# Sooner loads and one batch of logits in a convolution and mixture-of-experts kernel

## The chip, the cores and the metric

The kernel runs on one NeuronCore of a Trainium2 chip. The core has five engines with instruction streams of their own: TensorE (PE, with its weight loads shown as PEld), VectorE (DVE), ScalarE (ACT), GpSimd (POOL) and SyncE (SP, which here issues most of the loads). The metric is the device time of one launch, in microseconds (us); the figure of a kernel is the median of its runs.

## The reference

The first half is a dynamic convolution. For each of 8 x 2880 tokens with 192 channels in 8 heads, a softmax over 7 taps of `weight_gen` weights the token and its 6 predecessors:

```python
w = softmax(weight_gen)                       # (8, 2880, 8 heads, 7 taps)
x_unf = x_pad[:, idx, :].reshape(B, S, K, H, group)
out = np.einsum('bshk,bskhg->bshg', w, x_unf)
```

The second half is a mixture of 4 x 4 experts over the 23040 tokens. A softmax over 4 groups picks one group for each token, a softmax over its 4 experts picks one expert, and only that expert runs:

```python
h = np.maximum(xg[mask_e] @ w1[g, e], 0.0)    # 192 -> 1024
ye = h @ w2[g, e]                             # 1024 -> 192
out[tok_idx] = g_w * e_w * ye
```

All arrays are float32.

## The kernel before

The tokens are worked in 15 groups of 12 x 128. For a group, `load_group` loads the convolution weights (`wt`) and the inputs (`xin`); `softmax` normalises `wt`; `conv` makes the weighted sums on DVE; `route` computes the logits, picks the expert, ranks the tokens and gives each one a row in a DRAM buffer `rows`, which is sorted by expert. POOL writes the rows there by indirect DMA (`scatter_row`). After some groups `table` makes a list of blocks of one expert that are full; the ends of these rounds stand in `ROUNDS`. After the last group POOL also writes 16 blocks of padding (`rows<-pad`, line 588).

The experts run in visits, numbered from 0 in this text (the fourth is visit 3). A visit takes rows of one expert (`xb<-rows`), its first matrix (`wa`) and its second (`wc`). The first ten visits, 0 to 9, are "plain": 128 rows, float32 matmuls, and the first matrix is loaded straight into `wa`. The later ones take 256 rows and a "split" first matrix: it is loaded raw (`raw<-in_moe_w` and `raw<-w1lo`), ACT makes the high part (lines 806 and 809) and DVE the low part (line 824). For each of the three kinds of raw tile there are two, two and one buffers, so the raw tile of visit 12 is the one that visit 10 used. In the last rounds the second matrix is split as well (line 816). The last eight visits are plain again.

PE's work in a visit is `gemm1` (line 892, into `ph`), whose result ACT takes out with a relu (line 898, `hh`), and `gemm2` (line 919, into `py`), which ACT takes out (line 928) and POOL writes to `out` (line 936). Groups 0 to 4 sum the convolution in PSUM by transposing matmuls (line 319). From group 5 on DVE does the sums (lines 280 and 298), and the rows are transposed for the logits in six pairs (lines 393 and 394), each copied by ACT to a tile `xT`, of which there are two. After every second pair 8 logit matmuls follow (`logits`, line 365), with weights 32 columns wide; after the third such batch the result is copied, transposed back (line 430) and worked on by DVE.

Every engine runs its instructions in the order in which they were recorded. The code that records them is a planner: it keeps a clock for each engine (`clk`), advances it by a written cost for each step, and interleaves the visits with the steps of the convolution (`front`, `fill`, `step`) by it. Loads wait in a list `want`; `ask` puts a load there, `pump` issues those that are ready, in order, on SP. `ask_w` asks for the parts of a first matrix, `ask(n, 3)` for a second matrix, `ask(n, 0)` for the rows. `halves` (lines 623 to 636), in the early part, splits the tail rows of all first matrices through the same raw buffers and stores the low parts in DRAM.

Of the kernel before, what the change touches and what calls it, by code (L numbers as in the profile page):

```python
# [8 lines left out]
F32 = mybir.dt.float32  # L9
# [13 lines left out]
EVERY = {}  # L23
WHOLE = (99,) * 11 + (3, 0, 0)
TURNED = 10


class Slot:
# [4 lines left out]
def conv_moe_kernel(ctx: ExitStack, tc: tile.TileContext, x, wgen, w_group, w_expert, w1, w2, out):  # L33
# [5 lines left out]
    P = 128  # L39
# [163 lines left out]
    def run(eng, cost, *deps):  # L203
        clk[eng] = max([clk[eng]] + [d + HOP for d in deps]) + cost
        return clk[eng]
# [145 lines left out]
    def route(g, o):  # L351
# [26 lines left out]
        def forward():  # L378
            xTs = []
            for s2 in range(0, SG, 2):  # L380
                n, i = s2 // SC, s2 % SC // 2
                if o.chunks <= n:
                    yield Chunk(o, n + 1)
                row = xrow[n][:, s2 % SC:s2 % SC + 2, :]
                if i == 0:
                    rem = rt.tile([P, SC, HP], F32, name="rem")
                    nc.scalar.copy(out=rem, in_=xrow[n][:, :, P:D])
                    txT = run("act", 0.4, clk["dve"])
                    yield NEXT
                ttp = run("pe", 0.35, txT)  # L390
                tp = ps_t.tile([P, 3, P], F32, name="tp")
                for u in range(2):
                    nc.tensor.transpose(out=tp[:, u, :], in_=row[:, u, 0:P], identity=ident)  # L393
                nc.tensor.transpose(out=tp[:, 2, :], in_=rem[:, s2 % SC:s2 % SC + 2, :].rearrange("p s d -> p (s d)"), identity=ident)
                if len(xTs) == 2:
                    run("pe", 0.5, txT)
                    logits(s2 - 4, xTs)
                    xTs = []
                xT = rt.tile([P, 3, P], F32, name="xT", bufs=2)
                nc.scalar.copy(out=xT, in_=tp)  # L400
                txT = run("act", 0.48, ttp)
                xTs.append((xT, False))
                yield NEXT
            run("pe", 0.5, txT)
            logits(SG - 4, xTs)

        turned = 2 * g < TURNED
        if turned:
# [247 lines left out]
    def front():  # L656
# [5 lines left out]
        for g in range(ENDS[-1]):  # L662
# [2 lines left out]
            state["urgent"] = g == FIRST  # L665
            for n, c in enumerate(conv(g, o)):
                yield c
                if n in (2, 8) and 1 <= g < ENDS[-1] - 1:
                    load_group(g + 1, (n // 8,))
                if n >= (12 if state["slots"] else 4) and not o.ahead and g + 1 < ENDS[-1]:  # L670
                    o.ahead = True
                    side.append([softmax(g + 1), None])
# [288 lines left out]
    def blocks(n0, n1, paced):  # L961
        want, jobs = [], []

        def pump(upto=None):
            for a in list(want):
# [8 lines left out]
                want.remove(a)  # L974
                load(*a)

        def ask(n, part):
            if n < n1:
                want.append((n, part))

        def ask_x(n):
# [44 lines left out]
        if n0 + 2 < n1 and plain(n0 + 2):  # L1026
            ask_w(n0 + 2)
            ask(n0 + 2, 3)
        for n in range(n0, min(n0 + 3, n1)):
            ask(n, 0)  # L1030
        if n0 + 2 < n1 and not plain(n0 + 2) and (whole(n0 + 2) or whole(n0 + 1)):
# [15 lines left out]
        for i in range(len(units) + LAG):  # L1047
# [21 lines left out]
            if i < len(units):  # L1069
                n, j, u = units[i]  # L1070
                nb = blocks_of(n)
                at = j * NU + u
                end = at == nb * NU - 1
                if end and n + 3 < n1 and (plain(n + 3) or plain(n + 1)):
                    ask_w(n + 3)
                did = 0
                for job in list(jobs):
                    m, part, h = job
                    if m > n + 2 or (part == 3 and (m > n + 1 or at < LAG)):
                        continue  # L1080
                    must = end and m == n + 1
                    if not must and (did >= 1 or (m, part) in want or not ready(m)):
                        continue
                    jobs.remove(job)
                    work_split(job)
                    did += 1
                state["unit"] += 1
# [46 lines left out]
```

## Time and profile before

| | |
|---|---|
| runs | 1240.4, 1240.73 and 1241.85 us; median 1240.73 |
| profiled execution | 1243.13 us, of which 1241.5 us are the span of the trace |
| PE busy | 1190.0 us, 96% of the span |
| DVE busy | 922.6 us, 74% |
| ACT busy | 662.1 us, 53% |
| POOL busy | 428.0 us, 34% |
| DMA | 286.08 MB, 230 GB/s in the mean |

The span is read in stages. Up to about 115 us there are only convolution and routing; from there to about 239 us the plain visits run beside groups 2 to 5; from 239 to about 830 us the 256-row visits run beside the other groups; up to about 930 us the last routing follows; then come split visits alone, and plain ones at the end. Where PE is busy without a gap, PE's own instructions set the time. Where it stands, the row says in brackets for how long, and what released it. In the timeline a row is one instruction, or several equal ones that follow each other; "L892" is line 892 of the kernel before.

### The profile page before, as it was taken

To read this page: it belongs to the slowest core of one execution; us is meant where nothing else is said; L and a number is where in the kernel's file an instruction comes from. 1 tells how busy PE (TensorE), PEld (TensorE's weight loads), DVE (VectorE), ACT (ScalarE), POOL (GpSimd) and SP (SyncE) were. 2 spreads that over 40 slices of the span, in tenths; PEclk is the share of its full clock that TensorE was granted. 3 is DMA by queue.
4 is the path that set the end of the run, shared out by engine and by line. 5 is a ranking of instruction groups with operands and counts; after the bars stand their busy time and mean duration, and the time that the engine had idled before them with its cause. 6 is when DMAs were issued, how large, how long until landed. Compare 5 with 4: busy or idle time off the path is not lost.

```text
span 1241.5 us, 26600 instructions
## 1 busy us (share of the span) xinstructions
PE 1190.0 (96%) x9456; PEld 1162.9 (94%) x9456; DVE 922.6 (74%) x1582; ACT 662.1 (53%) x1242; POOL 428.0 (34%) x412
## 2 busy tenths in 40 slices
PE   5998899899999999999999999999998999999995
PEld 5887899899999999999999999999998999999995
DVE  8887678698989898898899889961255776777500
ACT  1223333455565555555656565555665777777531
POOL 3062424151626253433424342444154112211111
PEclk9999999899999999999999999999998999999998
DMA  4448988888877888797969786868569777776891
GB/s 150 137 137 245 271 289 263 251 248 268 245 259 232 274 237 265 214 295 222 282 204 301 218 279 206 238 199 259 179 188 300 226 224 232 221 224 199 233 261 43
DMA packets 181677, 286.08 MB, mean 230 GB/s; under 512 B 16084, under 2 KB 141775, under 8 KB 181280
## 3 DMA queue, kind: packets, MB, share of 16 engines
q1 hardware_dynamic: 162304, 245.09, 65.8%
q0 software_dynamic: 19232, 39.22, 9.6%
q8 instruction: 76, 1.25, 0.4%
q14 instruction: 65, 0.53, 0.1%
HBM read 240.89 MB, written 44.33 MB: 230 GB/s over the span
## 4 chain that ended last, share of the span: by engine, by line
PE 67%; issue 20%; DVE 4%; POOL 4%; DMA 3%; ACT 1%; SPq 0%; POOLq 0%; DVEq 0%; ACTq 0%
PE py L919 27%; PE ph L892 27%; POOL out L936 3%; PE pl L365 2%; PE ph L319 1%; PE py L214 1%; DVE pr L280 1%; PE py L319 1%; PE tpx L319 1%; PE tpx L868 1%; PE tpx L869 1%; PE tp L393 1%; DMA raw<-in_moe_w 1%; PE tp L374 1%; DMA wc<-in_moe_w 1%
## 5 line engine op out<-in xcount | busy, mean ns | idle before, releaser
L892 PE MATMUL ph<-xh,wa 128*128 128x256 f32 x2064 | 459.7, 299 | 0.0
L936 POOL DMA_INDIRECT out<-xb x190 | 207.2, 1090 | 657.3 <-ACT xb L928 407.5
L919 PE MATMUL py<-wc,hh 128*128 128x192 f32 x2240 | 417.7, 327 | 9.8 <-ACT xb L928 9.8
L919 PEld LDWEIGHTS py<-wc,hh 128*128 128x128 f32 x2240 | 359.9, 191 | 10.2 <-ACT xb L928 10.2
L892 PE MATMUL ph<-xlo,wa 128*128 128x256 f32 x1376 | 359.4, 283 | 0.0
L892 PEld LDWEIGHTS ph<-xh,wa 128*128 128x128 f32 x2064 | 351.0, 191 | 7.4 <-issue 5.9
L898 ACT ACTIVATE hh<-ph 128x512 f32<-128x512 f32 (+1 forms) x316 | 173.2, 548 | 317.2 <-PE ph L892 317.2
L892 PEld LDWEIGHTS ph<-xlo,wa 128*128 128x128 f32 x1376 | 262.5, 191 | 0.0
L280 DVE TENSOR_TENSOR pr<-xin,wt 128x1152 f32<-128x1152 f32 x190 | 253.6, 1351 | 6.2 <-PE tpx L319 6.1
L533 POOL DMA_INDIRECT rows<-xrow,posi x180 | 201.9, 1122 | 133.2 <-DVE posi L500 57.2
L298 DVE TENSOR_TENSOR xrow<-xrow,pr 128x1152 f32<-128x1152 f32 x120 | 162.4, 1353 | 0.6
L824 DVE TENSOR_TENSOR wa<-raw,wa 128x1024 fp32r<-128x1024 f32 x86 | 104.9, 1220 | 71.2 <-ACT wa L806 63.8
L921 PE MATMUL py<-wc,hh 128*128 128x384 f32 x400 | 122.5, 362 | 0.0
L824 DVE SCALAR_TENSOR_TENSOR hl<-ph,hh 128x512 fp32r<-128x512 f32 x100 | 69.1, 691 | 66.8 <-ACT hh L903 66.4
L922 PE MATMUL py<-wc,hl 128*128 128x192 f32 x400 | 100.8, 252 | 0.0
L806 ACT CAST wa<-raw 128x1024 fp32r<-128x1024 f32 x86 | 90.3, 1050 | 6.2 <-DMA raw<-in_moe_w 6.2
L809 ACT CAST wa<-raw 128x1024 fp32r<-128x1024 f32 x86 | 89.5, 1040 | 0.0
L928 ACT ACTIVATE xb<-py,xb 128x192 f32<-128x192 f32 x190 | 71.6, 420 | 27.3 <-PE py L919 21.5
L892 PE MATMUL ph<-xd,wa 96*128 96x128 f32 x576 | 78.8, 281 | 0.5 <-ACT xd L862 0.5
L922 PEld LDWEIGHTS py<-wc,hl 128*128 128x128 f32 x400 | 77.5, 194 | 0.0
L921 PEld LDWEIGHTS py<-wc,hh 128*128 128x128 f32 x400 | 76.2, 190 | 0.0
L892 PEld LDWEIGHTS ph<-xd,wa 96*128 96x128 f32 x576 | 75.1, 198 | 0.8 <-ACT xd L862 0.7
(165 smaller groups left out, 1291.2 us busy)
## 6 DMA issues: line engine op xcount, KB each, us to landing
wc<-in_moe_w SPq DMA_DIRECT2D x79, 768.0 KB
raw<-in_moe_w SPq DMA_DIRECT2D x86, 512.0 KB
raw<-in_moe_w SPq DMA_DIRECT2D x102, 256.0 KB
xin<-in_x SPq DMA_DIRECT2D x26, 864.0 KB
raw<-w1lo SPq DMA_DIRECT2D x86, 256.0 KB
raw<-in_moe_w SPq DMA_DIRECT2D x25, 768.0 KB
xb<-rows SPq DMA_DIRECT2D x86, 194.0 KB
wa<-in_moe_w SPq DMA_DIRECT2D x36, 384.0 KB
```

The costliest lines, as they stand in the source:

```text
L280: nc.vector.tensor_tensor(out=dst, in0=o.xin[:, c0 + k:c0 + k + SC, :].rearrange("p s (h g) -> p s h g", g=HG), in1=w4[:, c0:c0 + SC, :, k ...
L298: nc.vector.tensor_tensor(out=acc, in0=acc, in1=prs[k - 2], op=ALU.add)
L533: written_once(nc.gpsimd.indirect_dma_start(out=rows[:, :], out_offset=bass.IndirectOffsetOnAxis(ap=idx, axis=0), in_=src, in_offset=None, ...
L806: nc.scalar.copy(out=o.wa[:, 0, :], in_=o.raw[0])
L809: nc.scalar.copy(out=o.wa[:, 2, :], in_=o.raw[1])
L824: f(*a, **k)
L892: nc.tensor.matmul(ph[:, v, :], lhsT=w[:, f0:f0 + P], rhs=rhs, start=i == 0, stop=i == len(terms) - 1)
L898: nc.scalar.activation(out=hh, in_=ph, func=AF.Relu)
L919: nc.tensor.matmul(b.py[t][:, 0:D], lhsT=hh[:, v, c], rhs=wc[0][:, f, :], start=f == 0, stop=f == NFT - 1)
L921: nc.tensor.matmul(b.py[t], lhsT=hh[:, v, c], rhs=wc[f // 4][:, f % 4].rearrange("p l d -> p (l d)"), start=f == 0, stop=False)
L922: nc.tensor.matmul(b.py[t][:, 0:D], lhsT=hl[:, v, c], rhs=wc[f // 4][:, f % 4, 0, :], start=False, stop=f == NFT - 1)
L936: ins = nc.gpsimd.indirect_dma_start(out=out[:, :], out_offset=bass.IndirectOffsetOnAxis(ap=b.x.bitcast(I32)[:, t, D + 1:D + 2], axis=0), ...
```

## The change

There are four edits.

- In `front`, the weights and the first half of the inputs of the next group are asked for after the first product of a group instead of the third, for groups 2, 3 and 4. The second halves, and later groups, stay.
- In `blocks`, the second matrix of visit 3 is asked for at the start, with those of visits 0 to 2, and a set `asked` keeps it from being asked for twice.
- In `blocks`, the raw first matrices of visits 10 and 11 are asked for at the end of visits 6 and 7 instead of 7 and 8.
- In `route`, for groups 5 to 12, the first four transposed pairs go to tiles of the ring `hl` (four buffers, otherwise used early by the transposed convolution sums and late by the split visits), the last two to `xT`, and all 24 logit matmuls are issued together after the last pair.

```diff
--- before.py
+++ after.py
@@ -23,6 +23,7 @@
 EVERY = {}
 WHOLE = (99,) * 11 + (3, 0, 0)
 TURNED = 10
+BATCH = 13
 
 
 class Slot:
@@ -392,17 +393,21 @@
                 for u in range(2):
                     nc.tensor.transpose(out=tp[:, u, :], in_=row[:, u, 0:P], identity=ident)
                 nc.tensor.transpose(out=tp[:, 2, :], in_=rem[:, s2 % SC:s2 % SC + 2, :].rearrange("p s d -> p (s d)"), identity=ident)
-                if len(xTs) == 2:
+                if len(xTs) == 2 and g >= BATCH:
                     run("pe", 0.5, txT)
                     logits(s2 - 4, xTs)
                     xTs = []
-                xT = rt.tile([P, 3, P], F32, name="xT", bufs=2)
+                if g < BATCH and s2 < 8:
+                    xT = wp.tile([P, 3, P], F32, name="hl", bufs=4)
+                else:
+                    xT = rt.tile([P, 3, P], F32, name="xT", bufs=2)
                 nc.scalar.copy(out=xT, in_=tp)
                 txT = run("act", 0.48, ttp)
                 xTs.append((xT, False))
                 yield NEXT
-            run("pe", 0.5, txT)
-            logits(SG - 4, xTs)
+            run("pe", 0.25 * len(xTs), txT)
+            for q in range(len(xTs) // 2):
+                logits(SG - 2 * len(xTs) + 4 * q, xTs[2 * q:2 * q + 2])
 
         turned = 2 * g < TURNED
         if turned:
@@ -665,8 +670,9 @@
             state["urgent"] = g == FIRST
             for n, c in enumerate(conv(g, o)):
                 yield c
-                if n in (2, 8) and 1 <= g < ENDS[-1] - 1:
-                    load_group(g + 1, (n // 8,))
+                at = (0 if g < FIRST + 2 else 2, 8)
+                if n in at and 1 <= g < ENDS[-1] - 1:
+                    load_group(g + 1, (at.index(n),))
                 if n >= (12 if state["slots"] else 4) and not o.ahead and g + 1 < ENDS[-1]:
                     o.ahead = True
                     side.append([softmax(g + 1), None])
@@ -974,8 +980,11 @@
                 want.remove(a)
                 load(*a)
 
+        asked = set()
+
         def ask(n, part):
-            if n < n1:
+            if n < n1 and (n, part) not in asked:
+                asked.add((n, part))
                 want.append((n, part))
 
         def ask_x(n):
@@ -1026,6 +1035,8 @@
         if n0 + 2 < n1 and plain(n0 + 2):
             ask_w(n0 + 2)
             ask(n0 + 2, 3)
+            if n0 + 3 < n1 and plain(n0 + 3):
+                ask(n0 + 3, 3)
         for n in range(n0, min(n0 + 3, n1)):
             ask(n, 0)
         if n0 + 2 < n1 and not plain(n0 + 2) and (whole(n0 + 2) or whole(n0 + 1)):
@@ -1071,8 +1082,10 @@
                 nb = blocks_of(n)
                 at = j * NU + u
                 end = at == nb * NU - 1
-                if end and n + 3 < n1 and (plain(n + 3) or plain(n + 1)):
+                if end and n + 3 < n1 and plain(n + 3):
                     ask_w(n + 3)
+                if end and n + 4 < n1 and plain(n + 2) and not plain(n + 4):
+                    ask_w(n + 4)
                 did = 0
                 for job in list(jobs):
                     m, part, h = job
```

On SP the weights of group 4 stand as follows; `wt` and `xin` are that group's loads, `raw` and `w1lo` the loads and stores of `halves`. Before:

```order
L623 DMA raw_171<-in_moe_w 64x1024 x2
L636 DMA w1lo<-raw_170 64x1024 x2
L623 DMA raw_173<-in_moe_w 64x1024 x2
L636 DMA w1lo<-raw_172 64x1024 x2
L623 DMA raw_170<-in_moe_w 64x1024 x2
L238 DMA wt<-in_weight_gen 128x672
L248 DMA xin<-in_x 128x1728
```

Changed (the lines are those of the changed kernel, five or six higher further down):

```order
L628 DMA raw_171<-in_moe_w 64x1024 x2
L641 DMA w1lo<-raw_170 64x1024 x2
L628 DMA raw_173<-in_moe_w 64x1024 x2
L239 DMA wt<-in_weight_gen 128x672
L249 DMA xin<-in_x 128x1728
L641 DMA w1lo<-raw_172 64x1024 x2
L628 DMA raw_170<-in_moe_w 64x1024 x2
```

The two loads of group 4 have moved ahead of one store pair and one load pair. For groups 2 and 3 SP's order is the same as before.

A little later on SP come the raw first matrices of the first split visits; `raw_170` and `raw_172` are the buffers of visits 10 and 12, `raw_171` and `raw_173` those of visit 11. Before, the rows of visit 12 and then the first of visit 11:

```order
L786 ISA
L786 DMA raw_170<-in_moe_w 128x1024
L789 ISA
L789 DMA raw_172<-in_moe_w 64x1024
L789 ISA
L789 DMA raw_172<-w1lo 64x1024
L781 TENSOR_LOAD tab_1908
L781 ISA x2
L786 ISA
L786 DMA raw_171<-in_moe_w 128x1024
```

Changed, the rows of group 6's loads and of visit 11:

```order
L239 DMA wt<-in_weight_gen 128x672
L249 DMA xin<-in_x 128x1728
L787 TENSOR_LOAD tab_1908
L787 ISA x2
L792 ISA
L792 DMA raw_171<-in_moe_w 128x1024
L795 ISA
L795 DMA raw_173<-in_moe_w 64x1024
L795 ISA
L795 DMA raw_173<-w1lo 64x1024
```

Before, the load of visit 11 stands behind those of visit 12, which refill the buffers of visit 10. Changed, it stands directly behind the loads of group 6, ahead of the rows of visit 10, where the raw loads of visit 10 stood before; those have moved one visit further up.

The planner also places the last group's routing elsewhere among the visits. On POOL, the last scatters and the first block of padding; `xb` with its number is the buffer of a visit, and they go round from 158 to 165. Before:

```order
L936 DMA out<-xb_162 23040x192 x2
L533 DMA rows<-xrow,posi 188928x194 x12
L936 DMA out<-xb_163 23040x192 x2
L586 TENSOR_LOAD pfi
L586 ISA x2
L588 ISA
L588 DMA rows<-pad 128x388
```

Changed:

```order
L942 DMA out<-xb_159 23040x192 x2
L538 DMA rows<-xrow,posi 188928x194 x2
L942 DMA out<-xb_160 23040x192 x2
L538 DMA rows<-xrow,posi 188928x194 x10
L942 DMA out<-xb_161 23040x192 x2
L591 TENSOR_LOAD pfi
L591 ISA x2
L593 ISA
L593 DMA rows<-pad 128x388
```

The first padding stands behind the output of `xb_161` instead of that of `xb_163`, two visits sooner, and the output of one visit stands between the scatters.

## Rows read from the trace of the kernel before

**Rows 1.** The first part of the page (busy time, share of the span and instructions of each engine) and one line of its second part (PE's busy share in 40 equal slices of the span, in tenths).

```profile
PE 1190.0 (96%) x9456; PEld 1162.9 (94%) x9456; DVE 922.6 (74%) x1582; ACT 662.1 (53%) x1242; POOL 428.0 (34%) x412
...
PE   5998899899999999999999999999998999999995
```

**Rows 2.** Stretches of 50 us; columns: length of the stretch, then busy time and instructions of PE, PEld, DVE, ACT and POOL, the granted PE clock (1.00 is full speed), the share of time in which the DMA engines were busy, and GB/s.

```profile
100.00:150.00 50.00, 42.91 (x353) 39.75 (x351) 34.21 (x73) 15.15 (x37) 12.36 (x10) 0.93 0.86 241
...
200.00:250.00 50.00, 43.42 (x360) 41.55 (x359) 36.98 (x75) 21.15 (x45) 14.22 (x14) 0.93 0.86 259
...
300.00:350.00 50.00, 50.00 (x384) 49.16 (x386) 45.52 (x81) 29.09 (x54) 26.55 (x22) 1.00 0.82 255
...
900.00:950.00 50.00, 47.55 (x354) 46.95 (x352) 26.69 (x81) 28.11 (x50) 28.14 (x37) 0.99 0.79 247
950.00:1000.00 50.00, 49.20 (x364) 49.21 (x365) 35.41 (x51) 35.88 (x61) 10.41 (x11) 0.94 0.75 227
```

**Rows 3.** Timeline, 123 to 136 us; columns: start, length, engine (SPq is SP's DMA queue), line, operation, tiles, count, and in brackets the idle time before and what ended it.

```profile
123.22 1.25 SPq L636 DMA_DIRECT2D w1lo<-raw  x2
...
126.56 0.58 SPq L238 DMA_DIRECT2D wt<-in_weight_gen  x1
...
132.56 0.85 DVE L255 TENSOR_REDUCE m<-wt 128x96 f32<-128x672 f32 x1 [7.99 <-DMA wt<-in_weight_gen]
...
134.34 0.76 ACT L258 ACTIVATE wt<-wt 128x672 f32<-128x672 f32 x1 [5.83 <-DVE wt L257]
...
136.00 0.92 PE L919 MATMUL py<-wc,hh 128*128 128x192 f32 x4 [4.19 <-ACT xb L928]
```

**Rows 4.** The three standstills of PE and what follows each, as stretches; columns as in rows 2.

```profile
131.81:136.00 4.19, 0.00 (x2) 0.00 (x1) 3.37 (x6) 1.66 (x5) 0.00 (x0) 1.00 1.03 280
136.00:140.30 4.30, 4.30 (x22) 4.28 (x23) 4.20 (x12) 0.22 (x1) 2.66 (x2) 0.60 1.05 232
228.97:234.57 5.60, 0.01 (x2) 0.00 (x1) 1.10 (x1) 2.18 (x5) 0.00 (x0) 0.81 1.05 259
234.57:239.30 4.73, 4.73 (x18) 4.73 (x19) 4.31 (x7) 1.68 (x4) 0.97 (x1) 0.51 0.81 257
947.22:950.80 3.58, 0.33 (x2) 0.14 (x2) 1.54 (x3) 2.90 (x6) 2.55 (x3) 0.78 1.05 354
950.80:956.00 5.20, 5.20 (x22) 5.20 (x23) 2.95 (x6) 3.63 (x6) 1.26 (x2) 0.50 0.76 233
```

**Rows 5.** Timeline, 209 to 235 us, the loads of raw first matrices by SP, and the first work on visit 11's by ACT; columns as in rows 3.

```profile
209.56 1.48 SPq L786 DMA_DIRECT2D raw<-in_moe_w  x1
...
221.99 0.34 SPq L786 DMA_DIRECT2D raw<-in_moe_w  x1
...
224.84 0.35 SPq L786 DMA_DIRECT2D raw<-in_moe_w  x1
...
232.39 1.04 ACT L806 CAST wa<-raw 128x1024 fp32r<-128x1024 f32 x1 [6.17 <-DMA raw<-in_moe_w]
```

**Rows 6.** The chain of waits, early and at 285 us; columns: start, length, engine, tile, line, count. L365 are the logits; 8 matmuls are 16 instructions, 24 are 48.

```profile
110.63 1.49 PE pl L365 x48
...
284.93 0.57 PE pl L365 x16
```

**Rows 7.** Timeline of PE's weight loads: the last before and the first behind a batch of 24 logit matmuls, and the same for a batch of 8; columns as in rows 3.

```profile
211.02 1.18 PEld L214 LDWEIGHTS py<-ident 128*128 128x128 f32 x11 [0.53 <-ACT xlo L325]
...
213.82 0.31 PEld L374 LDWEIGHTS tp<-ident,hl 128*128 128x128 f32 x3 [0.20 <-issue]
...
284.55 0.14 PEld L394 LDWEIGHTS tp<-ident,rem 128*128 128x128 f32 x1
...
285.43 0.30 PEld L892 LDWEIGHTS ph<-xh,wa 128*128 128x128 f32 x2 [0.20 <-issue]
```

**Rows 8.** Timeline of POOL, ACT and PE around the padding, 928 to 951 us; columns as in rows 3.

```profile
928.87 3.27 POOL L588 DMA_DIRECT2D rows<-pad  x6
...
947.51 0.54 POOL L588 DMA_DIRECT2D rows<-pad  x1 [0.75 <-issue]
...
947.90 0.83 ACT L816 CAST wc<-raw 128x768 fp32r<-128x768 f32 x1 [6.98 <-DMA raw<-in_moe_w]
...
948.27 0.33 PE L868 MATMUL tpx<-ident,xb 128*128 128x128 f32 x1 [1.05 <-DMA xb<-rows]
950.80 0.47 PE L869 MATMUL tpx<-ident,xd 128*128 128x128 f32 x1 [2.20 <-ACT xd L852]
```

**Rows 9.** A stretch of 10 us during the padding; columns as in rows 2.

```profile
930.00:940.00 10.00, 10.00 (x80) 10.00 (x80) 7.45 (x15) 7.37 (x13) 6.28 (x11) 1.00 1.05 320
```

**Rows 10.** SP's semaphore waits at line 770, the loads of rows (count, shortest, median and longest in ns, first and last start); the first three loads of rows; the stretch from 98 to 108 us; and PE's first use of such rows.

```profile
L770 SPq EVENT_SEMAPHORE  x117: 17/28/9524, 98.3 to 1208.2; - x117
...
107.92 3.10 SPq L770 DMA_DIRECT2D xb<-rows  x3
...
98.00:108.00 10.00, 9.25 (x79) 8.54 (x80) 8.99 (x10) 3.65 (x5) 3.68 (x3) 1.00 0.88 260
...
115.36 0.43 PE L860 MATMUL tp<-ident,xb 128*96 128x128 f32 x2 [0.57 <-ACT xrow L375]
```

**Rows 11.** Waits between 240 and 900 us: who waited for whom, us in total, times, longest.

```profile
DVE wa L824 <- ACT wa L806: 51.5, 16, 10.0
```

## Prediction

> **What bounds the kernel now.** I read the page first: PE is busy 1190.0 us of a span of 1241.5, in nearly every slice 90% or more [rows 1]. So PE's own instructions set the time, and apart from start and end there is little idle time to win. The stretches of 50 us say where it is: from 300 to 350 us PE is busy without a gap, while 100 to 150, 200 to 250 and 900 to 1000 us lack 7.1, 6.6, 2.5 and 0.8 us [rows 2]. The timeline puts nearly all of the last three, and 4.2 us of the first, into three standstills, and a table of stretches gives each with what follows it: 4.19, 5.59 and 3.25 us (3.58 less the 0.33 in which PE worked) [rows 4]. Behind each one PE is busy, but at a granted clock of 0.60, 0.51 and 0.50, that is mostly or all at 1.2 instead of 2.4 GHz. At half clock the same instructions take twice as long, so these stretches hold a further loss of 4.30 x 0.40 = 1.7, 4.73 x 0.49 = 2.3 and 5.20 x 0.50 = 2.6 us.
>
> The sum below is made in the profiled execution, 1243.1 us: the span and 1.6 us around it. That is 2.4 us over the median of 1240.73; I take the 2.4 us off at the end.
>
> **The weights of group 4.** DVE waited 7.99 us for `wt`, which SP issued at 126.56 us [rows 3]. The exponential at line 258 stood next on ACT, which takes its instructions in order, so the outputs of PE behind it were not taken out, and PE stood until 136.00. In the changed order the load stands ahead of one store pair and one load pair, where SP stood at 123.22: 3.3 us sooner. The load itself has the same work queued before it, so I let all behind it come 3.3 us sooner and PE stand for about 0.9 us. Whether so short a stop still brings the slow clock, rows 3 and 4 do not tell; I take half of its 1.7 us. Term: 3.3 + 0.9 = 4.2 us. Bounds: 0, if SP reaches this place later, and 5.9, if the stop goes with its slow clock. For groups 2 and 3 the order on SP is unchanged, so the edit gives nothing there.
>
> **The second matrix of visit 3.** 768 KB more are now queued ahead of the first rows `xb`. SP's own time for it is covered: it waited up to 9.5 us, from 98.3 us on, before those rows could be issued at 107.92 [rows 10]. The transfer takes 768 KB / 260 GB/s = 3.0 us more of the DMA engines, which are 0.88 busy there. PE first uses such rows at 115.36, over 7 us behind the issue, and there it waited for ACT, not for them. I count nothing; without that cover it would be at most these 3.0 us, by pushing everything on SP back. In exchange 768 KB are gone from the stretch where `wt` was late, 1.03 to 1.05 busy [rows 4]. The Trainium skill, "DMA: Bandwidth & Descriptors", section "Queues, rings and completion order", says that each DMA engine consumes the descriptors of one issuing engine's ring in order. That rule speaks against this edit: by it the rows of visits 0 to 2 wait for the whole matrix. No row here separates the two, and by the rule the sum is the same as long as the slack at 115.36 holds.
>
> **The raw matrices of visits 10 and 11.** Before, visit 11's load stood behind that of visit 12, which had to wait until visit 10's buffers were free: SP issued these at 221.99, and visit 11's only at 224.84 [rows 5]. ACT met line 806 with nothing landed, stood 6.17 us until 232.39, and everything behind it on ACT too; PE stood 5.59 us [rows 4]. In the changed order visit 11's load stands where visit 10's stood, at 209.56, some 15 us sooner. Even a landing as slow as the 7.5 us from 224.84 to 232.39 would end at 217, long before ACT is free at 232.39 - 6.17 = 226.2. The rows and the second matrix of visit 10 stand behind one such load, as before. Those of visit 9 now stand behind visit 10's raw load, 1024 KB, at 259 GB/s [rows 2] 4.0 us of transfer; they are asked for three visits ahead, and I count nothing for them. Next in line are line 806 itself (1.04 us) and PE's own instructions. Term: 5.6 + 2.3 = 7.9 us. Bounds: 5.6, if the slow clock comes all the same, to 7.9.
>
> **Logits of groups 5 to 12.** No instruction is removed, but the 24 matmuls are in one batch. The timeline of the weight loads has both kinds: from the end of the last load before a batch of 8 (284.69) to the first behind it (285.43) 0.74 us, around a batch of 24 (212.20 to 213.82) 1.62 us [rows 7]. Three batches cost 2.22, one costs 1.62: 0.60 us a group, and 4.8 us for eight groups, since PE has no gap there [rows 2]. Bounds: 4.0 to 5.0, for the units in which the batches stand differ. The copies to `hl` and `xT` are as many as before, and the last batch waited for the last copy before, too.
>
> What a logit matmul costs inside a batch is seen in the chain: 48 instructions take 1.49 us, 31 ns each [rows 6]. The Trainium skill, "TensorE: Matmul & The Clock Gate", section "Part 3: Packing small matmuls", has matmuls in different column strips of the array run beside each other, about 4 ns apart. By that a batch of 24 would cost little more than one of 8, and a group would save 2 x 0.74 = 1.5 us instead of 0.6, eight groups 11.8. The trace shows 31 ns and not 4, so the sum goes by the row.
>
> **The padding.** This comes with the planner's new order. Before, the 16 blocks of padding were written from 928.87 to 948 us, with the DMA engines 1.05 busy [rows 8, 9]; ACT waited 6.98 us for a raw second matrix and PE 1.05 us for rows, then 2.20 for ACT. Now the first block stands two visits sooner, beside visits whose second matrices are not split and are asked for three visits ahead. It may cost nothing there: 3.25 + 2.6 = 5.9 us gained. It may cost the same: 0. It may also hit twice: -5.9. No row shows padding beside such visits; the sooner loads make me take the middle of the upper half, 3.0 us.
>
> **Sum.** 4.2 + 7.9 + 4.8 + 3.0 = 19.9 us. 1243.1 - 19.9 = 1223.2, less 2.4: 1220.8 us, 1.6% faster. The start up to 115 us and the end are untouched, and after each term PE is bound by itself again, so I expect nothing of it to be taken back.
>
> **The rivals.**
> - Part of it is not gained: group 4's weights come no sooner, because SP and the scatters run late behind visit 3's matrix, and the padding costs what it did. For it: SP issues in order and the DMA engines are 0.88 busy [rows 10]. Against: the 7 us of slack at 115.36. Then 7.9 + 4.8 = 12.7 us are left: 1228.0.
> - The sooner raw loads only exchange one late transfer for another: PE arrives 10 us sooner in a stretch where the DMA engines are 1.05 busy [rows 4], so a second matrix or rows of visits 10 to 12 are late instead. It would give back half of the 7.9, and with the terms of the first rival gone leave 8.7: 1232.0. Against it: a share of 0.86 over the 50 us [rows 2].
> - Slower: VectorE becomes the bound. Routing steps have moved among the products, so the low parts of a visit (line 824) could end after PE needs them, once in each of groups 5 to 12, beside the 256-row visits. For it: DVE is busy 45.5 of 50 us there [rows 2]. Against: DVE itself waits 51.5 us for ACT at that very line [rows 11], so it is ahead, and it has the same instructions as before. Each stop, priced as the third standstill with its slow clock, is 5.9 us; from the third on, 17.7 us, they outweigh the first three terms (16.9). Eight would give 1220.8 + 3.0 + 47.2 = 1271.0.
> - The logits of one batch pack closer, so that a batch of 24 costs as much as one of 8, 0.74 us: 11.8 instead of 4.8 us are saved, 1213.8. Against it: the early batches of 24 take 1.62 [rows 7].
> - The change does not do what it says: the sooner loads wait on SP for their buffers and issue when they did. Then the logits alone are left: 1235.9. Against it: the raw buffers are last used by `halves`, before these visits.
>
> **How the numbers follow.** Chances: the forecast 0.60, the first rival 0.18, the second 0.09, waiting buffers 0.04, closer logits 0.01, VectorE 0.05, and 0.03 for something that eats all of it to within 0.2%. 0.2%, about 2.5 us, is what a measurement of this kernel can tell from no change. The forecast's own range is 1216 to 1227: all upper bounds together are 24.7 us, and the lower ones of the raw loads and the logits, with the padding as before, leave 4.2 + 5.6 + 4.0 = 13.8. For 8 in 10 it is widened over the first two rivals and, at the other end, to the closer logits: 1214 to 1232. Faster by more than 0.2%: 0.92; within 0.2%: 0.03; slower: 0.05.
>
> **What would show it.** Right: near 130 us DVE's wait for `wt` is some 4 us instead of 8 and PE's stop under 1.5; near 215 to 225 us ACT's line 806 has no wait for a raw load, and no slow clock follows; in the 256-row stretch there is one batch of 48 logit instructions a group; the padding runs some 20 us sooner relative to the visits, with under 2 us of idle PE. Wrong: `wt` issued at 126 us or later; a wait of PE for `wc`, `xb` or line 824 that is not there before; a batch that costs over 2 us; a standstill of over 3 us around the padding.

## The result: 1218.8 us, and the profile after

The changed kernel takes 1218.8 us in the median of six runs (1217.2 to 1219.5), the kernel before beside it 1240.8 (1240.4 to 1241.9). The ratio is 0.9819, with a 95% interval of 0.9807 to 0.9832: 22 us, or 1.8%, faster. The forecast was 1220.8 with a range of 1214 to 1232.

The gain is that of this chip. Some of the experiments fell on two other chips, on which every run, those of the kernel before included, took 1342 to 1388 us; PE stands there for 137 to 151 us in all in the traces of changed kernels (the kernel before was not traced there). On one of them the changed kernel took 1375.3 us and the kernel before 1375.2. These experiments are named as such below, and their times say nothing on the steps.

The first part of the page and the granted clock in 40 slices, for the changed kernel:

```profile
PE 1176.0 (97%) x9456; PEld 1154.3 (95%) x9456; DVE 921.1 (76%) x1582; ACT 661.3 (54%) x1242; POOL 445.3 (37%) x412
PEclk9999999999999999999999999999999999999998
```

Against [rows 1] the span is 23.8 us shorter (1241.5 to 1217.7). PE is busy 14.0 us less (1190.0 to 1176.0) with the same 9456 instructions, and outside its work 9.8 us less passes (51.5 to 41.7). So both happened that the prediction spoke of: PE stands less, and it works faster where it ran at half clock. The same stretches of 50 us as in [rows 2] (length, busy time and instructions of PE, PEld, DVE, ACT and POOL, granted clock, DMA share, GB/s):

```profile
100.00:150.00 50.00, 44.42 (x393) 41.05 (x392) 36.94 (x76) 17.81 (x40) 15.57 (x12) 1.00 0.90 264
200.00:250.00 50.00, 49.01 (x414) 47.55 (x413) 46.73 (x85) 27.42 (x55) 20.54 (x20) 1.00 1.00 295
300.00:350.00 50.00, 50.00 (x407) 49.23 (x406) 46.65 (x74) 28.27 (x52) 25.16 (x21) 1.00 0.86 262
900.00:950.00 50.00, 50.00 (x385) 50.00 (x384) 30.31 (x44) 35.54 (x62) 16.58 (x21) 1.00 0.84 246
950.00:1000.00 50.00, 50.00 (x392) 50.00 (x391) 35.19 (x52) 36.14 (x64) 9.72 (x10) 1.00 0.78 227
```

From 200 us on nothing is left but 1 us of short pauses around the routing, and the clock is 1.00 in every stretch of this table; of the slices only the last falls below nine tenths.

**Group 4's weights.** The load on SP, DVE's first use, and PE's stop (start, length, engine, line, operation, tiles, count, idle time before and its releaser), then the stop and what follows it as stretches:

```profile
122.35 0.59 SPq L239 DMA_DIRECT2D wt<-in_weight_gen  x1
129.03 0.85 DVE L256 TENSOR_REDUCE m<-wt 128x96 f32<-128x672 f32 x1 [5.96 <-DMA wt<-in_weight_gen]
132.47 0.76 PE L925 MATMUL py<-wc,hh 128*128 128x192 f32 x3 [2.16 <-ACT xb L934]
211.84 0.55 PE L375 MATMUL tp<-ident,xlo 128*128 128x128 f32 x3 [0.57 <-ACT xrow L376]
```

```profile
130.31:132.47 2.16, 0.00 (x0) 0.00 (x0) 2.13 (x5) 1.66 (x5) 0.00 (x0) 1.00 1.07 307
132.47:137.00 4.53, 4.53 (x36) 4.51 (x37) 4.43 (x12) 0.70 (x3) 2.81 (x2) 1.00 0.77 175
```

The load is issued 4.2 us sooner than in [rows 3], DVE's wait is 5.96 instead of 7.99 us, and PE goes on at 132.47 instead of 136.00. The stop of 2.16 us brings no half clock, where the 4.19 us of [rows 4] did. The last row of the timeline serves as a mark further on: a transpose that PE reached at 216.06 us before (its row stands below, with the group weights alone).

**The raw matrices.** SP issues visit 11's at 205.32 instead of 224.84 [rows 5], and ACT's first work on it starts without a wait; the second standstill is gone:

```profile
205.32 0.34 SPq L792 DMA_DIRECT2D raw<-in_moe_w  x1
221.90 1.04 ACT L812 CAST wa<-raw 128x1024 fp32r<-128x1024 f32 x1
```

```profile
220.00:230.00 10.00, 10.00 (x79) 9.80 (x78) 8.59 (x20) 6.60 (x14) 0.97 (x1) 1.00 1.05 300
```

**The logits.** Weight loads of PE around a batch of 24 in a 256-row visit, and the batch in the chain of waits (start, length, line, count):

```profile
399.32 1.29 PEld L925 LDWEIGHTS py<-wc,hh 128*128 128x128 f32 x8
400.84 0.81 PEld L366 LDWEIGHTS pl<-hl,wr 128*32 128x32 f32 x32 [0.23 <-issue]
402.28 0.30 PEld L898 LDWEIGHTS ph<-xh,wa 128*128 128x128 f32 x2 [0.20 <-issue]
```

```profile
400.91 1.45 PE pl L366 x48
```

From the end of the last load before the batch (399.32 + 1.29 = 400.61) to the first behind it (402.28) pass 1.67 us, about the 1.62 of the early batches in [rows 7]. Read in the same way, all eight batches of groups 5 to 12 take 1.67 us. In the kernel before, the first two batches of a group take 0.74 to 0.75 us each and the third 0.79 to 0.80, as this one (289.86 + 1.29 = 291.15, to 291.94):

```profile
289.86 1.29 PEld L919 LDWEIGHTS py<-wc,hh 128*128 128x128 f32 x8
291.94 0.30 PEld L892 LDWEIGHTS ph<-xh,wa 128*128 128x128 f32 x2 [0.20 <-issue]
```

Three batches of 8 are thus 2.28 us, one of 24 is 1.67: 0.61 us a group, 4.9 us for eight groups.

**The padding.** POOL's first and last blocks, and ACT's two longest waits for raw second matrices (line 822, before 816):

```profile
891.89 2.21 POOL L593 DMA_DIRECT2D rows<-pad  x4
911.70 0.54 POOL L593 DMA_DIRECT2D rows<-pad  x1 [0.80 <-issue]
925.86 0.83 ACT L822 CAST wc<-raw 128x768 fp32r<-128x768 f32 x1 [2.56 <-DMA raw<-in_moe_w]
935.87 0.83 ACT L822 CAST wc<-raw 128x768 fp32r<-128x768 f32 x1 [2.81 <-DMA raw<-in_moe_w]
```

It begins 37 us sooner than in [rows 8], ACT's waits stay under 3 us where the longest was 6.98, and the third standstill is gone. Counted from ACT's first work on a raw second matrix (903.01 us here, 920.63 before), the padding runs from 11 us ahead to 9 behind, where it ran from 8 to 27 us behind.

### The profile page after: what moved, and what is told of

Read it like the earlier page. It is cut to its first block, busy times and chain, and to the rows that moved or that the text cites. A ratio compares the mean times of both kernels' runs of the same rounds, so it can differ in the third digit from the quotient of the medians.

```text
span 1217.7 us, 26611 instructions
## 1 busy us (share of the span) xinstructions
PE 1176.0 (97%) x9456; PEld 1154.3 (95%) x9456; DVE 921.1 (76%) x1582; ACT 661.3 (54%) x1242; POOL 445.3 (37%) x412
## 3 DMA queue, kind: packets, MB, share of 16 engines
q8 instruction: 76, 1.25, 0.4%
## 4 chain that ended last, share of the span: by engine, by line
PE 88%; DVE 4%; issue 2%; DMA 2%; ACT 1%; SPq 1%; POOL 0%; POOLq 0%; DVEq 0%; ACTq 0%
PE ph L898 38%; PE py L925 29%; PE py L927 6%; PE py L928 3%; DVE pr L281 2%; PE pl L366 2%; PE tpx L875 2%; PE tpx L874 2%; PE ph L320 1%; PE tp L394 1%; DMA xb<-rows 1%; PE py L215 1%; DMA wa<-in_moe_w 1%; PE tpx L320 1%; PE py L320 1%
## 5 line engine op out<-in xcount | busy, mean ns | idle before, releaser
L942 POOL DMA_INDIRECT out<-xb x190 | 222.7, 1172 | 610.0 <-ACT xb L934 351.4
L830 DVE TENSOR_TENSOR wa<-raw,wa 128x1024 fp32r<-128x1024 f32 x86 | 105.0, 1220 | 48.6 <-ACT wa L812 40.6
L830 DVE TENSOR_TENSOR xlo<-tpx,xh 128x512 fp32r<-128x512 f32 x86 | 59.2, 689 | 27.8 <-ACT xh L879 27.8
L898 PE MATMUL ph<-xd,wa 96*128 96x128 f32 x576 | 76.2, 275 | 0.5 <-ACT xd L868 0.5
```

What stands on the lines that cost most here:

```text
L830: f(*a, **k)
L898: nc.tensor.matmul(ph[:, v, :], lhsT=w[:, f0:f0 + P], rhs=rhs, start=i == 0, stop=i == len(terms) - 1)
L942: ins = nc.gpsimd.indirect_dma_start(out=out[:, :], out_offset=bass.IndirectOffsetOnAxis(ap=b.x.bitcast(I32)[:, t, D + 1:D + 2], axis=0), ...
```

## The experiments

**Each edit alone.** The four edits separate cleanly, and each was put into the kernel before by itself. Logits alone (`BATCH`, the tiles `hl`, the loop over the pairs; its core):

```diff
-                if len(xTs) == 2:
+                if len(xTs) == 2 and g >= BATCH:
...
+            for q in range(len(xTs) // 2):
+                logits(SG - 2 * len(xTs) + 4 * q, xTs[2 * q:2 * q + 2])
```

> The kernel before with the logit edit alone; nothing is left out of the computation. In its order of instructions the 16 padding blocks already stand where they stand in the changed kernel (behind the 126th store of results instead of the 130th). Theory (the padding's gain belongs to this edit, since the shorter batches pull the routing ahead): the logits give 8 x 0.60 = 4.8 us and the third standstill with its half clock goes, 5.9 us, together 10.7: 1230.1 us; the two stops near 130 and 230 us stay (about 4.2 and 5.6 us), the one near 945 us is absent. Rival 1 (the padding is only free because the raw loads or PE's place have moved, too): 4.8 us, 1236.0, and a stop of 3 us or more near 943 us. Rival 2 (part of the changed kernel's saving in the batched stretch comes from the other edits): less than 4 us in that stretch.

Measured: 1229.6 us, ratio 0.9902 (0.9884 to 0.9920), 11.3 us faster. The theory holds; the batches take 1.67 us here too, so the second rival (less than 4 us there) falls as well. The stretches at the first two standstills, and where the padding (902 to 922 us) runs:

```profile
130.26:133.58 3.32, 0.00 (x0) 0.00 (x0) 3.25 (x6) 1.66 (x5) 0.00 (x0) 0.83 1.02 251
133.58:138.00 4.42, 4.42 (x18) 4.33 (x19) 4.32 (x12) 0.22 (x1) 2.79 (x2) 0.50 1.04 250
227.65:231.99 4.34, 0.01 (x2) 0.00 (x1) 1.10 (x1) 2.13 (x4) 0.00 (x0) 0.94 1.05 259
231.99:237.00 5.01, 5.01 (x19) 5.01 (x20) 4.35 (x7) 1.84 (x4) 0.97 (x1) 0.50 1.03 314
910.00:920.00 10.00, 10.00 (x75) 10.00 (x74) 3.71 (x5) 7.13 (x12) 5.88 (x9) 1.00 0.82 270
```

Both early stops are there with half clock behind them; from 910 to 920 PE works without a gap, and there is no stop behind that either. So the third standstill goes by the logit edit alone, through the planner's new order; the two early stops are shorter in this execution than in [rows 4]. PE reaches the transpose that serves as a mark 1.3 us sooner than in the kernel before (216.06), although the order up to there is the same:

```profile
214.74 0.55 PE L375 MATMUL tp<-ident,xlo 128*128 128x128 f32 x3 [0.57 <-ACT xrow L376]
```

Raw matrices alone (with the set `asked`):

```diff
-                if end and n + 3 < n1 and (plain(n + 3) or plain(n + 1)):
+                if end and n + 3 < n1 and plain(n + 3):
                     ask_w(n + 3)
+                if end and n + 4 < n1 and plain(n + 2) and not plain(n + 4):
+                    ask_w(n + 4)
```

> The kernel before with the edit of the raw first matrices of visits 10 and 11 alone; nothing is left out. Theory: the stop of 5.59 us and the 2.3 us of half clock behind it go, 7.9 us: 1232.9 us, with the raw load of visit 11 issued near 209 us and the other two standstills as before. Rival (the loads only exchange one late transfer for another, and what covers them in the changed kernel is the sooner start of everything by the other edits): a new stop of 2 us or more between 215 and 250 us, a gain of 4 us or less, 1236.8 or more.

Measured: 1233.2 us, ratio 0.9929 (0.9907 to 0.9950), 7.8 us faster, as the theory had it. No transfer takes the lost one's place, and the third standstill is there:

```profile
222.00:232.00 10.00, 10.00 (x80) 10.00 (x79) 9.32 (x19) 5.98 (x14) 1.80 (x2) 1.00 0.95 271
938.77:943.11 4.34, 0.33 (x2) 0.14 (x2) 1.53 (x3) 2.89 (x6) 2.51 (x3) 0.79 1.03 349
```

Group weights alone:

```diff
-                if n in (2, 8) and 1 <= g < ENDS[-1] - 1:
-                    load_group(g + 1, (n // 8,))
+                at = (0 if g < FIRST + 2 else 2, 8)
+                if n in at and 1 <= g < ENDS[-1] - 1:
+                    load_group(g + 1, (at.index(n),))
```

> The kernel before with the edit of the group weights' load alone; nothing is left out. Theory: SP issues the weights of group 4 about 3.3 us sooner, near 123.3 us, and PE goes on near 132.7 instead of 136.0; with the half clock behind the stop (1.7 us) staying or going that is 3.3 to 5.0 us: 1235.7 to 1237.4. The half clock at 116 us, before the edit's place, stays. Rival (the second matrix of visit 3 is what makes room on SP): under 2 us, 1239 or more.

Measured: 1239.7 us, ratio 0.9992 (0.9978 to 1.0006): 1.3 us, not to be told from none. By the time the rival seems right, by the trace the theory. SP's load and the stops with what follows:

```profile
122.37 0.61 SPq L238 DMA_DIRECT2D wt<-in_weight_gen  x1
211.78 0.55 PE L374 MATMUL tp<-ident,xlo 128*128 128x128 f32 x3 [0.57 <-ACT xrow L375]
```

```profile
132.14:132.70 0.56, 0.00 (x1) 0.01 (x1) 0.56 (x2) 0.56 (x3) 0.00 (x0) 1.00 1.05 241
132.70:137.00 4.30, 4.30 (x34) 4.28 (x35) 4.20 (x12) 0.60 (x2) 2.66 (x2) 1.00 1.05 223
943.40:948.63 5.23, 0.48 (x3) 0.19 (x2) 1.54 (x3) 2.90 (x6) 2.21 (x3) 0.76 0.97 350
948.63:954.00 5.37, 5.37 (x26) 5.37 (x27) 2.95 (x6) 4.12 (x7) 1.43 (x2) 0.60 0.51 140
```

The load is issued at 122.37, the stop is 0.56 us, no half clock follows, and PE reaches the transpose at 211.78 us, 4.28 us sooner than in the kernel before, whose row is:

```profile
216.06 0.55 PE L374 MATMUL tp<-ident,xlo 128*128 128x128 f32 x3 [0.57 <-ACT xrow L375]
```

The third standstill is then 5.23 - 0.48 = 4.75 us long instead of 3.25: PE came sooner, the transfer it waits for did not come as much sooner. There PE goes on at 948.63 instead of 950.80, so 2.2 of the 4.3 us are left.

Second matrix of visit 3 alone (with the set `asked`):

```diff
+            if n0 + 3 < n1 and plain(n0 + 3):
+                ask(n0 + 3, 3)
```

> The kernel before with the sooner load of visit 3's second matrix alone; nothing is left out. Theory: one load pair's time on SP is gone between 111 and 126 us, so the weights of group 4 are issued 0 to 1 us sooner, and that is all: 1239.7 to 1240.7. Rival 1 (the transfer is paid for: 768 KB ahead of the first rows): up to 3.0 us slower, 1243.7. Rival 2 (the half clock at 116 us, which the changed kernel lacks, goes by this edit): 1.7 us more, 1238.0 to 1239.0, with a granted clock of 1.0 there.

Measured: 1241.5 us, ratio 1.0002 (0.9987 to 1.0018): no gain and no loss in the time. In its execution the first stop is 2.76 us and the second 6.58:

```profile
130.49:133.25 2.76, 0.00 (x1) 0.00 (x0) 2.69 (x6) 1.66 (x5) 0.00 (x0) 1.00 1.02 291
133.25:138.00 4.75, 4.75 (x37) 4.73 (x38) 4.64 (x13) 0.92 (x3) 2.81 (x2) 1.00 0.35 95
224.99:231.57 6.58, 0.00 (x1) 0.00 (x1) 1.10 (x1) 2.18 (x5) 0.00 (x0) 0.69 0.97 256
```

PE reaches the mark nearly as soon as with the group weights alone, 3.98 us sooner than before:

```profile
212.08 0.55 PE L374 MATMUL tp<-ident,xlo 128*128 128x128 f32 x3 [0.57 <-ACT xrow L375]
```

The second stop is then longer by 1.0 us than in [rows 4], and at the end of the span 1.9 us are left (1239.6 instead of 1241.5). That the first stop is shorter is not this edit's doing for certain: from the issue of the first rows to that of the weights SP takes 17.2 us in this kernel and 17.2 in the one with the logits alone, whose order on SP is that of before up to there. With that same order it takes 18.6 in the kernel before and 19.2 with the raw matrices alone; it takes 14.7 with the group weights alone and 14.5 in the changed kernel. The granted clock at 118 us is 1.00 here, but see the last section.

The product of the four ratios is 0.9826, within the interval of the whole. So the times do not show that the edits are worth more together than one by one.

**The padding put back.** In the changed kernel its table is worked out later, so that it is issued behind the 130th and 132nd store again:

```diff
-        if last:
-            pfi = t("pfi", (P, NE), I32)
-            v.tensor_tensor(out=pfi, in0=cnt.rearrange("p e o -> p (e o)"), in1=lower, op=ALU.add)
...
         if last:
+            for _ in range(7):
+                yield NEXT
+            pfi = t("pfi", (P, NE), I32)
+            v.tensor_tensor(out=pfi, in0=cnt.rearrange("p e o -> p (e o)"), in1=lower, op=ALU.add)
             for e in range(NE):
```

> The changed kernel with the 16 padding blocks put back behind the 130th and 132nd store of results, once more; the order on the other engines stays as changed, nothing is left out. Where the kernel before takes its 1241 us, theory (the padding's place alone made the third standstill): PE stops for 3 to 5 us in all near 920 us, waiting for rows and for a second matrix, half clock behind it, 1224 to 1226 us. Rival (PE's place against the routing, which the batches also moved, made it): no stop over 1 us there, 1218 to 1220. Where the kernel before takes 1350 us or more and PE stands for over 100 us in all, neither can be read from the time, and only the stretch behind the padding is looked at.

Measured: 1220.7 us, ratio 0.9846 (0.9819 to 0.9873). That is 1.9 us above the changed kernel, with intervals that overlap; the 5.9 of the theory do not come, nor the rival's zero in the trace. The first block of padding and ACT's two longest waits, then the stretches of padding and of PE's stops:

```profile
904.82 0.59 POOL L594 DMA_DIRECT2D rows<-pad  x1 [2.60 <-issue]
925.57 0.84 ACT L823 CAST wc<-raw 128x768 fp32r<-128x768 f32 x1 [3.93 <-DMA raw<-in_moe_w]
936.47 0.84 ACT L823 CAST wc<-raw 128x768 fp32r<-128x768 f32 x1 [4.07 <-DMA raw<-in_moe_w]
```

```profile
912.00:926.00 14.00, 14.00 (x111) 14.00 (x111) 9.18 (x13) 7.38 (x13) 7.71 (x12) 1.00 1.05 343
926.00:930.00 4.00, 3.55 (x29) 3.33 (x28) 3.07 (x5) 4.00 (x8) 2.64 (x3) 1.00 0.96 281
938.50:939.40 0.90, 0.10 (x2) 0.03 (x1) 0.90 (x3) 0.90 (x4) 0.00 (x0) 1.00 0.91 219
```

The DMA engines are 1.05 busy as in [rows 9], ACT waits up to 4.07 us for raw second matrices instead of 2.81, but PE stands only 0.45 and 0.80 us, and the clock stays at 1.00. What differs is the last scatters of the routing. In the kernel before, the first and the last of them were

```profile
911.28 0.97 POOL L533 DMA_INDIRECT rows<-xrow,posi  x1 [0.61 <-DVE posi L500]
925.35 0.97 POOL L533 DMA_INDIRECT rows<-xrow,posi  x1 [0.31 <-issue]
```

and the padding followed from 928.87 on: the scatters ran from 9 us ahead of ACT's first work on a raw second matrix to 6 us behind it, and the padding from 8 us behind it. With the padding put back the last scatter is

```profile
886.53 0.98 POOL L538 DMA_INDIRECT rows<-xrow,posi  x1 [0.30 <-issue]
```

and ends 17 us ahead of the padding and 14 us ahead of ACT's first work on a raw second matrix (901.33). The padding itself begins 3.5 us behind that work, against 8.2 before, so its place is near the old one but not the same. The scatters are not shown to be the cause: the second matrix that ACT waited 6.98 us for in the kernel before was issued 11 us behind the last of them, and landed some 10 us later (ACT's work on it starts at 947.90 [rows 8]):

```profile
937.56 0.40 SPq L793 DMA_DIRECT2D raw<-in_moe_w  x1
```

With the padding put back the load behind the longest wait is issued at 930.08 and used at 936.47, 6.4 us later. PE's place against the routing, the rival of the expectation, also stays as changed in this kernel, so it is not told apart from the scatters.

The first run of this kernel fell on one of the other chips:

> The changed kernel with one thing put back: the 16 padding blocks are issued behind the 130th and 132nd store of results, as in the kernel before, instead of behind the 126th and 128th (their table is worked out that much later on VectorE; the order on the other engines stays). Nothing is left out. Theory (the padding's place alone made the third standstill): PE stops for 3 to 5 us in all near 920 us, waiting for rows and for a second matrix, half clock behind it, and the time is 5.9 us above the changed kernel's 1218.8: 1224 to 1226. Rival (the standstill came from PE's place against the routing, which the batches also moved, and the padding is not the cause): no stop, 1218 to 1220.

It took 1365.1 us, the kernel before 1351.2 (ratio 1.0118, 1.0077 to 1.0159): neither the theory nor the rival can be read from it, and there this kernel is slower than the one before.

**What group 4's weights are worth in the changed kernel.** These runs and a try at a better version fell on the two other chips.

> The changed kernel once more, beside the next three on the same chip, as the mark that they are measured against: 1217 to 1220 us; if the kernel before spreads over 8 us here as it did beside the first four experiments, this one spreads over less, since the stops that differ from execution to execution are gone.

Measured: 1375.3 us, the kernel before 1375.2, ratio 1.0002 (0.9971 to 1.0033). The page's first line, and what ACT waited for (line, count, busy time, mean; idle time and releasers):

```profile
PE 1220.9 (89%) x9456; PEld 1186.3 (87%) x9456; DVE 922.4 (67%) x1582; ACT 663.2 (48%) x1242; POOL 436.8 (32%) x412
```

```profile
L904 ACT ACTIVATE hh<-ph 128x512 f32<-128x512 f32 (+1 forms) x316 | 173.3, 549 | 392.5 <-PE ph L898 250.8 <-remote 95.8 <-issue 18.3
```

Outside its work PE loses 1370.2 - 1220.9 = 149.3 us, against 41.7 above. ACT waits 95.8 us for something that the profile does not name ("remote"). The kernel before took 1375 us at one time and 1351 at another on the same chip, so ratios within 1% are not read here, and the forecast of 1217 to 1220 us cannot be checked.

Without the group weights' edit, twice, and without visit 3's second matrix:

> The changed kernel with the edit of the group weights' load taken back; nothing is left out of the computation. Alone, that edit moved PE's going on from 136.0 to 132.7 us and PE was still 4.4 us ahead behind the second standstill, but the median moved only 1.3 us. Theory (the gain was eaten by the padding's standstill, which came later and longer by 1.5 us there; where that standstill is gone the local gain is kept): weights issued at 124.5 to 126.5 us, PE stopped 3 us or more, and the median 3 to 5 us above the changed kernel's: 1222 to 1224. Rival (the edit is worth what it showed alone): 1.3 us above, 1220.

> The changed kernel with the edit of the group weights' load taken back, once more, beside the run with the padding put back; nothing is left out. Theory (the edit is worth its local gain of 3.3 to 4.4 us once the later standstills are gone, and showed 1.3 alone because the padding's standstill took it): weights issued at 124.5 to 126.5 us, PE stopped 3 us or more, the median 3 to 5 us above 1218.8: 1222 to 1224. Rival (with visit 3's second matrix loaded sooner the weights come 1.5 us sooner anyway, so that the edit is worth 1 to 2): 1220 to 1221.

> The changed kernel without the sooner load of visit 3's second matrix; nothing is left out. Theory (the two edits before group 4's weights overlap: with the weights' load put ahead, one load pair less on SP matters no more): weights issued at 122.4 us as in the changed kernel, the same stop of about 2 us or less, the median within 1 us of the changed kernel's: 1218 to 1220. Rival 1 (the edit brought the weights 1.5 us sooner by itself, and that adds): 1220 or more. Rival 2 (its transfer costs more than it saves): 1217 or less.

Measured: 1376.1 us (ratio 1.0017), 1360.3 (1.0075) and 1374.9 (1.0018). From the first rows to the weights SP took 17.7 and 17.2 us without the group weights' edit, 14.8 without the second matrix, and 13.3 with both: on SP the edit does what it says. What it brings in time stays open. Without both:

> The changed kernel with both edits taken back that bring group 4's weights sooner (their own load, and the sooner second matrix of visit 3); nothing is left out. Alone these two moved the median by 1.3 us and by nothing, though each trace showed PE about 4 us ahead at 211 us. Theory (what PE was ahead was spent at the two later standstills, which this kernel lacks, so together they are worth the first term, 4.2 us): weights issued at 124.5 to 126.5 us, one stop of 3 to 5 us near 130 us with half clock behind it, 1222 to 1224 us against 1218.8. Rival (the stop in the one profiled execution of before was longer than it mostly is, and the two edits are worth what they showed alone): 1219.5 to 1220.5.

Measured: 1361.7 us, the kernel before 1350.2, ratio 1.0083 (1.0054 to 1.0111). Open as well; the ratio lies above 1, if by less than 1%. The exponential later:

```diff
-                if n >= (12 if state["slots"] else 4) and not o.ahead and g + 1 < ENDS[-1]:
+                if n >= (12 if state["slots"] else 6 if g == FIRST + 1 else 4) and not o.ahead and g + 1 < ENDS[-1]:
```

> The changed kernel, but the reduction and the exponential over group 4's weights stand two products of the convolution later on VectorE and ACT; nothing is left out. Theory (what is left near 130 us is DVE's and then ACT's wait for these weights, with nothing else late): the stop of 2.16 us and the small one of 0.51 behind it go, 1216.0 to 1217.0 us. Rival (the later exponential is then late for its own use, or the stop only moves to the next late transfer): a stop of over 1 us elsewhere between 130 and 170 us, 1218.8 or more.

Measured: 1378.8 us, ratio 1.0050 (1.0018 to 1.0082). No better version is shown.

## Why the prediction was right, point by point

- **The raw loads** (7.9): right, in size too. 5.59 us of standing and the half clock behind are gone, and alone they are worth 7.8 us in the median. The rival of an exchanged late transfer falls.
- **The logits** (4.8): right, in size too. Three batches of 8 cost 2.28 us, one of 24 costs 1.67: 0.61 us a group, 4.9 for eight, within the bounds. The chain gives 1.45 us for 48 instructions, 30 ns each, so the closer logits fall. The Trainium skill, "TensorE: Matmul & The Clock Gate", "Part 3: Packing small matmuls", has matmuls in different column strips start about 4 ns apart; this trace does not show it.
- **Group 4's weights** (4.2): the lead is as forecast, the picture of it only in part. PE reaches the same transpose at 211.84 in the changed kernel and at 216.06 before, 4.2 us. But it is made up otherwise: PE went on 3.5 us sooner, none of the 1.7 us of half clock came where I took half, and 1.0 us was lost again before the transpose, 0.5 of it in a wait for rows. That this gives 4.2 once more is luck. Two signs of being right did not come: DVE's wait was 5.96 us and not some 4, and the stop left was 2.16 us and not under 1.5; PE came to it 1.5 us sooner than before (130.31 instead of 131.81). The kernels with the logits alone and the raw matrices alone, which are the one before up to here, stopped for 3.32 and 5.31 us, so one execution's 4.19 is one value of several. Nor is the lead this edit's alone: the second matrix of visit 3 by itself gave 3.98 us at the same transpose, and the unchanged order 1.3 in another execution. Alone, the edit moved the median 1.3 us, and in its trace PE spent part of its lead at the next late transfer. That all of it is kept in the changed kernel, where no late transfer is left behind it, is argued from the trace and was not timed. Together with the padding this takes away the first rival, 1228.0.
- **Visit 3's second matrix** (0): right in the time, and no loss either. The lead in its trace was not forecast; whether the edit makes it is open.
- **The padding** (3.0): mis-sized, and the cause was half named. Nothing of the standstill is left, so 3.25 us and the 2.6 of half clock, 5.9, were gained: the upper bound. "The sooner loads make me take the middle" was the step that failed; the loads were no part of it, since the logit edit alone does it. Its 11.3 us are 4.9 and 5.9 and 0.5 that is not assigned. The padding's own place is worth the stops of 1.25 us in the trace, and 1.9 us in the median, which is not clear of noise. The rest falls, by subtraction, to what else the new order moved: the scatters in front of the padding and PE's place against the routing. Neither was tried by itself, so the cause of most of this standstill stays open.

In sum: 4.2 + 7.9 + 4.9 + 5.9 = 22.9 of the 23.8 us between the two profiled executions; the forecast was 19.9. The profiled execution of before lay 2.3 us over its median, as taken off, that of the changed kernel 0.5. VectorE never became the bound: PE has no gap from 250 to 1200 us.

## What to carry to other kernels

Price a standstill with the half clock behind it, and look for the next late transfer before you count a lead: time won ahead of it was partly spent waiting there. That such edits pay only together is likely by the traces, but the times do not show it. Where an edit lets a planner reorder, read the new order on every queue; here a saving of 4.9 us on PE came with 5.9 more, through the new order that the planner made. And a stop in one profiled execution is one draw: with the same order up to it, the stop at one place was 3.3 to 5.3 us long.

## What was not expected of the hardware

- The stops of 0.56, 2.16 and 2.76 us were followed by a clock of 1.00 (2.4 GHz), those of 3.32, 4.34, 5.48 and 6.58 us by 0.50 (1.2 GHz), and those of 4.19, 5.31 and 5.59 us by 0.60, 0.60 and 0.51. But half clock also came without a stop of this kind: behind three pauses of 0.46 to 0.57 us from 113.7 to 116.4 us it is there in the kernel before and in two others, and not in the changed kernel with the same pauses:

```profile
116.40:118.40 2.00, 2.00 (x10) 2.00 (x11) 1.77 (x6) 0.14 (x1) 0.00 (x0) 0.50 0.78 295
```

```profile
116.40:118.40 2.00, 2.00 (x18) 2.00 (x19) 1.86 (x6) 0.39 (x1) 0.00 (x0) 1.00 0.57 213
```

- That half clock cost nothing that can be told: when PE goes on near 130 us hangs on the weights, and a PE that comes later stops for less. With the group weights alone, which have it, the stop was 0.56 us and PE went on at 132.70 us; the changed kernel, without it, stopped for 2.16 us and went on at 132.47. With SP's order of before, the kernel before (with it) stopped for 4.19 us and went on at 136.00, those with the raw matrices alone and the logits alone (without it) stopped for 5.31 and 3.32 us and went on at 135.61 and 133.58.
- The 336 KB of weights took 6.7 us from issue to first use in one execution and 4.9 in another (122.35 to 129.03; 121.35 to 126.26 with the padding put back), beside equal orders on SP.
- The change is worth 1.8% where PE sets the time. On a chip where the traced kernels stood for over 100 us it was worth nothing (1.0002), and the variants of the changed kernel that were run there had ratios of 1.002 to 1.012 to the kernel before; none was faster. What stops the engines there the profile does not name.
